# Half-tile sums, value tiles loaded once, and weight preparation moved: an attention, SiLU and squared-ReLU chain on one core

## The chip, the core and the metric

The kernel runs on one core of a Trainium2 chip. The metric is the device time of one execution in microseconds (us); lower is better. The core has a matrix engine (PE, TensorE), a vector engine (DVE), a scalar engine (ACT), GpSimd (POOL) and a sync engine (SP), which here issues nearly every transfer between HBM and the on-chip memory. Each engine works through its own instructions in the order in which they stand; an instruction that waits for another engine or for a transfer holds up everything behind it on its engine.

## The reference

```
def _attn_ref(q, k, v):                       # 4 batches, 8 heads, 576 positions, 64 wide
    ...
    mask = (rel >= 0) & (rel < window)        # window 128
    scores = np.where(mask, scores + bias[None], -1000000000.0)
    ...
    return np.matmul(attn, v)
def _moe_ref(x, w_in, w_out):                 # 2304 tokens, 512 -> 2048 -> 512
    h = x @ w_in
    g = h * (1.0 / (1.0 + np.exp(-h)))
    return g @ w_out
def _moe2_ref(x, w_in, w_out):                # the same sizes
    h = np.maximum(x @ w_in, 0.0)
    return h * h @ w_out
```

The output is the second layer applied to the first layer applied to the attention output, all in float32.

## The kernel before, in words

Every float32 operand of a large product is held as two parts, a high one (a rounded copy, written by ACT) and a low one (the difference, written by DVE or POOL), and a product is three matmuls: high by high, high by low, low by high. The 2304 tokens form four blocks of 512 (0 to 3) and one narrow block of 256 (4). The work has four phases; the code numbers its steps by n within each.

- **Phase one** (n from 0 to 71, `mm1`, L651 and L640) multiplies by the first layer's w_in. The attention of the later blocks is interleaved up to n = 55 (scores L303, transposes L387, values L433). Results pass `act1` on ACT and `act2` on DVE (L674) and are stored to HBM as `g0d`. Steps 64 to 71 work on the narrow block with two accumulators each, joined by ACT (L663) and DVE (L664).
- **Phase two** multiplies by the first layer's w_out. Blocks 0 and 1 do so directly (`mm2`, L815, n from 0 to 31): `load_g` fetches a piece of `g0d`, `split_g` makes its two parts (ACT L798, DVE L799), PE does twelve matmuls. Blocks 2 and 3 use seven products of sums instead of eight (`mm2_seven`, L746, pairs p from 16 to 31, two steps each); these need sums of w_out's quarters and of `g0d`. The narrow block follows directly (n from 64 to 71, L815 again).
- **Phases three and four** are the second layer in the same seven-product form (L875, then L970).

A weight tile `(layer, in or out, i)` is 1 MB. `prepare` takes one from HBM, repairs its words (`w_first` on DVE L482, `w_scale` on ACT L487, `w_join` on DVE L491), builds the quarter sums (`w_sums`, DVE L511 to L524) and stores the result back to HBM (`w_put`, L531, or `w_put_parts`, L555); a later phase gets it again (`w_get`, L538). For the first layer's w_out the parts are made at once (`w_hi`, and `w_lo` L502 on POOL) and stay on chip; its sums go to HBM in a whole 1 MB tile and come back in phase two, one tile at a time, into the single `raw` buffer, where `w_sums_hi` (ACT L588) and `w_sums_lo` (DVE L592) split them.

SP issues all transfers in the order of the code. A transfer also waits until the one eight places before it on the queue has landed, as the eight queue semaphores are used in turn.

Of the kernel before, what the change touches and what calls it, by code (L numbers as in the profile page):

```python
# [8 lines left out]
F32 = mybir.dt.float32  # L9
# [15 lines left out]
def kernel(  # L25
# [37 lines left out]
    wd0 = tc.dram_tile([P, NF // 2, 16 * P], F32, name="wd0")  # L63
# [41 lines left out]
    def attention(ap, ps, n0):  # L105
# [157 lines left out]
        def load_v(u):  # L263
            if double(u):
                return load_double_v(u)
            _, _, b, t0, n, m0, hp = units[u]
            t = ap.tile([P, 2, P], F32, tag="v", name="v", bufs=4)
            if m0 == n:
                nc.sync.dma_start(
                    out=t, in_=v[b, hp, t0 - m0:t0 + n, :].rearrange("(k p) d -> p k d", p=P)  # L270
                )
            else:
                if m0:
                    nc.sync.dma_start(out=t[:m0, 0], in_=v[b, hp, t0 - m0:t0, :])
                nc.sync.dma_start(out=t[:n, 1], in_=v[b, hp, t0:t0 + n, :])
            xv[u] = [t[:, 0], t[:, 1]]
# [222 lines left out]
    def w_lo(x, chunks=(0, 1)):  # L499
        w = w_t[x]  # L500
        for a in chunks:
# [7 lines left out]
    def w_sums(x):  # L509
# [9 lines left out]
        else:  # L519
# [4 lines left out]
            tt(low[:, 3], high[:, 0], low[:, 2], ALU.subtract)  # L524

# [205 lines left out]
    def mm2_seven(p, some_, pools):  # L731
# [4 lines left out]
            [ws_t[0, 1, i][:, y, 2 * P * j:2 * P * (j + 1)] for j in range(4)]  # L736
# [16 lines left out]
    def evacuate_second(b, step):  # L753

        acc = acc_t[0, b]
        c11, c12, u, c22 = e1
# [24 lines left out]
    def load_g(n):  # L781
        if n < NS:
            if "n" not in places:
                places["n"] = x_p.tile([P, 16 * P], F32, tag="xa", name="l")
            t = places["n" if n < 2 * FIRST else "l"][:, n % 4 * BLK:(n % 4 + 1) * BLK]
# [5 lines left out]
    def split_g(n):  # L791
        if n < NS:
            t, at_ = l_t.pop((0, n)), n % 3 * 2 * BLK
# [276 lines left out]
    def prepare(phase, x, place, n):  # L1070

        then(phase, n - 3, lambda: w_load(x, place(I32)))
        then(phase, n, w_first, x)
        then(phase, n, w_scale, x)
        then(phase, n + 1, w_join, x)
        then(phase, n + 2, w_sums, x)
# [6 lines left out]
        then(phase, n + 5, w_put_parts, x)  # L1083

# [12 lines left out]
    with tc.manual_schedule():  # L1097
# [5 lines left out]
        with tc.tile_pool(name="at", bufs=2) as ap, tc.tile_pool(  # L1103
# [511 lines left out]
```

## Time and profile before

| what | value |
| --- | --- |
| time, median of 3 runs | 883.37 us (881.88 to 885.65) |
| the profiled execution's own time | 881.42 us |
| its span, first to last instruction | 879.6 us |
| PE busy | 851.4 us (97%) |
| DVE busy, ACT busy, POOL busy | 619.4 us, 461.5 us, 135.9 us |
| mean granted PE clock, as a share of full speed | 0.992 |
| moved by DMA | 205.08 MB, 233 GB/s on average |

PE busy is the union of its matmuls; the ends of matmuls are modelled, so short waits between matmuls can hide in it. The granted clock is 1.00 (2.4 GHz) or 0.50 (1.2 GHz) at any moment; a window's figure is the mean.

### The profile page before, as it was taken

Reading aid. Unit: us, or ns where it says so; the run is one execution under the profiler, and the core shown is the slowest. Engines: PE = TensorE matmul, PEld = TensorE weight load, DVE = VectorE, ACT = ScalarE, POOL = GpSimd, SP = SyncE. Lnnn points to the kernel's source line nnn. Section 1 sums busy time; section 2 is a strip of 40 time slices with the busy share of each in tenths; the row PEclk is TensorE's granted clock in tenths of the full one; section 3 lists DMA queues with packets and bytes.
Section 4 is the critical chain, followed back from the end, with each engine's and each line's share of the span. In section 5 each row is a group of like instructions: output and inputs, shape, how many; then the busy total and the mean of one; then the engine's idle time right before and its main releaser. Section 6 shows DMA issues by size and latency. Waiting matters only on the chain.

```text
span 879.6 us, 17249 instructions
## 1 busy us (share of the span) xinstructions
PE 851.4 (97%) x6296; PEld 769.4 (87%) x6296; DVE 619.4 (70%) x1302; ACT 461.5 (52%) x925; POOL 135.9 (15%) x208
## 2 busy tenths in 40 slices
PE   8999999899999999998999799999999999999998
PEld 7678787687888887778999699999999999999998
DVE  6766686856765575667993356684957789998884
ACT  8788685657643553334332246665666543344331
POOL 6675432452631000000000000000000000000000
PEclk9999999999999999999999899999999999999999
DMA  9676799999967599993466826649477953444431
GB/s 276 205 228 206 222 326 312 311 363 324 341 233 251 178 345 415 400 348 123 142 224 232 287 72 206 226 168 321 165 250 271 313 192 127 151 140 144 132 109 48
DMA packets 126324, 205.08 MB, mean 233 GB/s; under 512 B 12704, under 2 KB 87712, under 8 KB 121632
## 3 DMA queue, kind: packets, MB, share of 16 engines
q1 hardware_dynamic: 125968, 203.86, 68.6%
q8 instruction: 49, 0.80, 0.4%
q14 instruction: 35, 0.29, 0.1%
q10 hardware_dynamic: 272, 0.13, 0.1%
HBM read 126.88 MB, written 77.07 MB: 232 GB/s over the span
## 4 chain that ended last, share of the span: by engine, by line
PE 78%; DMA 12%; DVE 5%; ACT 2%; issue 2%; SPq 1%; POOL 1%; DVEq 0%; ACTq 0%; POOLq 0%
PE acc L970 20%; PE h L651 18%; PE a L875 10%; PE acc L746 8%; DMA raw<-wd 5%; PE d L875 5%; PE acc L815 4%; PE b L875 3%; PE h L640 3%; PE o L433 2%; DMA spare<-in_w_dram 2%; PE s L303 1%; DMA l<-g0d 1%; PE so L303 1%; PE pp L387 1%
## 5 line engine op out<-in xcount | busy, mean ns | idle before, releaser
L651 PE MATMUL h<-x,w 128*128 128x512 f32 x768 | 184.8, 397 | 1.5 <-DVE t L674 1.5
L970 PE MATMUL acc<-w,g 128*128 128x256 f32 x1372 | 182.3, 283 | 1.0 <-DVE g L942 0.6
L970 PEld LDWEIGHTS acc<-w,g 128*128 128x128 f32 x1372 | 175.0, 192 | 1.6 <-DVE g L942 0.8
L651 PEld LDWEIGHTS h<-x,w 128*128 128x128 f32 x768 | 142.7, 189 | 35.9 <-DVE st L329 2.2
L815 PE MATMUL acc<-gx,w 128*128 128x512 f32 (+1 forms) x512 | 116.1, 387 | 8.8 <-DVE gx L799 7.2
L815 PEld LDWEIGHTS acc<-gx,w 128*128 128x128 f32 x512 | 93.6, 194 | 31.0 <-DVE gx L799 9.9
L935 ACT CAST g<-lay 128x1024 fp32r<-128x1024 f32 x36 | 37.9, 1052 | 96.0 <-issue 51.1
L875 PE MATMUL a<-x,w 128*128 128x384 f32 x432 | 80.9, 335 | 0.7 <-ACT t L1520 0.7
L356 POOL TENSOR_SCALAR z<-z,st 128x192 f32<-128x192 f32 (+1 forms) x104 | 65.3, 644 | 91.5 <-DVE st L350 47.3
L875 PEld LDWEIGHTS a<-x,w 128*128 128x128 f32 x432 | 75.3, 188 | 1.2 <-ACT t L1520 1.0
L674 DVE SCALAR_TENSOR_TENSOR t<-t,h 128x512 f32<-128x512 f32 x64 | 43.7, 683 | 27.3 <-ACT t L669 27.0
L669 ACT ACTIVATE t<-h 128x512 f32<-128x512 f32 x64 | 38.3, 598 | 37.6 <-PE h L651 35.8
L746 PE MATMUL acc<-x,w 128*128 128x256 f32 x392 | 56.1, 283 | 0.5 <-DVE lay L1024 0.5
L746 PEld LDWEIGHTS acc<-x,w 128*128 128x128 f32 x392 | 52.3, 192 | 0.8 <-DVE lay L1024 0.7
L339 ACT ACTIVATE z<-z,st 128x192 f32<-128x192 f32 (+1 forms) x104 | 45.5, 440 | 7.1 <-DVE st L329 7.0
L798 ACT CAST gx<-l 128x512 fp32r<-128x512 f32 x40 | 24.3, 623 | 42.6 <-DMA l<-g0d 29.7
L487 ACT ACTIVATE spare<-spare 128x1024 f32<-128x1024 f32 x25 | 29.2, 1166 | 26.6 <-DMA spare<-in_w_dram 26.6
L746 PE MATMUL acc<-g,w 128*128 128x256 f32 x140 | 40.4, 289 | 2.7 <-DVE g L724 2.7
L502 POOL TENSOR_TENSOR w<-spare,w 128x512 fp32r<-128x512 f32 x28 | 39.1, 1415 | 22.1 <-ACT w L497 22.0
L799 DVE TENSOR_TENSOR gx<-l,gx 128x512 fp32r<-128x512 f32 x40 | 27.4, 688 | 20.1 <-ACT gx L798 19.8
L970 PE MATMUL acc<-w,gx 128*128 128x256 f32 x140 | 39.6, 283 | 0.0
L942 DVE TENSOR_TENSOR g<-lay,g 128x1024 fp32r<-128x1024 f32 x26 | 31.9, 1225 | 9.2 <-ACT g L935 7.0
(195 smaller groups left out, 1469.0 us busy)
## 6 DMA issues: line engine op xcount, KB each, us to landing
g0d<-t SPq DMA_DIRECT2D x72, 256.0 KB, 5.9
lay<-g1d SPq DMA_DIRECT2D x72, 256.0 KB, 3.3
spare<-in_w_dram SPq DMA_DIRECT2D x34, 512.0 KB, 8.0
raw<-wd SPq DMA_DIRECT2D x15, 1024.0 KB, 7.0
wd<-spare SPq DMA_DIRECT2D x12, 1024.0 KB, 8.0
l<-g0d SPq DMA_DIRECT2D x40, 256.0 KB, 7.1
g1d<-t SPq DMA_DIRECT2D x50, 192.0 KB, 3.7
g1d<-lay SPq DMA_DIRECT2D x46, 192.0 KB, 3.8
```

The costliest lines, as they stand in the source:

```text
L339: nc.scalar.activation(z[r, j, k], z[r, j, k], AF.Exp, bias=least[r, j:j + 1], scale=-1.0, accum_out=total[r, j:j + 1],)
L356: nc.gpsimd.tensor_scalar(z[r, j, k], z[r, j, k], share[r, j:j + 1], 1.0, ALU.mult, ALU.mult)
L502: nc.gpsimd.tensor_tensor(w[:, 1, a], words(x)[1][:, a].bitcast(F32), w[:, 0, a].bitcast(F32), ALU.subtract)
L651: nc.tensor.matmul(h[:, j * w:(j + 1) * w], lhsT=wi[:, wh, c * P:(c + 1) * P], rhs=x[xh][:, c, :w], start=c == 0 and i == 0, stop=c == KC ...
L669: nc.scalar.activation(t_t[n], h_t[n], AF.Tanh, scale=0.5)
L674: nc.vector.scalar_tensor_tensor(t, t, 1.0, h, ALU.add, ALU.mult)
L746: nc.tensor.matmul(acc[name][:, m], lhsT=w[y][j][:, m * P:(m + 1) * P], rhs=g1[(p - FIRST) % 3][x][:, k], start=i == 0 and m == 0 and z == ...
L815: nc.tensor.matmul(to, lhsT=wo[:, a, c * P:(c + 1) * P], rhs=rhs, start=f == 0 and i == 0, stop=f == NF - 1 and i == len(both) - 1, skip_g ...
L875: nc.tensor.matmul(acc[to], lhsT=w[wh][:, c * P:(c + 1) * P], rhs=o[:, xh, c], start=r in (0, 1, 3) and c == 0 and k == 0, stop=c == 1 and ...
L935: nc.scalar.copy(g[0][:, :, :4], l_t[1, d])
L942: tt(g[1][:, :, :4], a, g[0][:, :, :4].bitcast(F32), ALU.subtract)
L970: nc.tensor.matmul(acc[to][:, half], lhsT=g[x], rhs=w[y], start=i == 0 and half == 0 and j == 0, stop=i == NI - 1 and j == 2, skip_group_c ...
```

## The change

- The sums of the first layer's w_out are written as a half tile over the upper half of the raw tile, in another order, and kept as 512 KB. Phase two gets them two at a time, side by side in one `raw` buffer (`get_sums` at n = 3, 9, 15 and 21, used at 7 and 8, 13 and 14, 18 and 19, 25 and 26). `w_lo` of these tiles becomes one DVE instruction in place of two on POOL.
- Value tiles of the attention are loaded one 128 by 128 block at a time and a block is used by both units that need it. A unit issues one transfer as before, of 64 KB in place of 128 KB for 36 units.
- Five weight tiles are prepared near the end of phase one: (0,1,7) as before, and (1,0,4) to (1,0,7), of which two were prepared in mid phase one and two in phase two. They lie in `raw` and in the buffers `lay` and `gx`, whose pools now open at n = 55 in place of after phase one.
- Loads of weight tiles are asked four or five steps ahead of use in place of three. `load_l`, the sums and parts for the seven products, `load_g` of the narrow block, `split_g` of it and `load_x2` stand earlier in the code; slots of buffers are renumbered to allow it. In phase three the preparation of (1,1,5), (1,1,6) and (1,1,7) moves by 6, 7 and 1 steps.

The core of the diff (block indentation that only moved is left out):

```
-    wd0 = tc.dram_tile([P, NF // 2, 16 * P], F32, name="wd0")
+    wd0 = tc.dram_tile([P, NF // 2, 8 * P], F32, name="wd0")
...
+            for t in (t0 - m0, t0):
+                if (b, hp, t) not in c:
+                    c[b, hp, t] = ap.tile([P, P], F32, tag="v", name="v", bufs=8)
+                    nc.sync.dma_start(out=c[b, hp, t], in_=v[b, hp, t:t + P, :])
+            xv[u] = [c[b, hp, t] for t in (t0 - m0, t0)]
...
     def w_lo(x, chunks=(0, 1)):
         w = w_t[x]
+        if x[1]:
+            nc.vector.tensor_tensor(
+                w[:, 1], words(x)[1].bitcast(F32), w[:, 0].bitcast(F32), ALU.subtract
+            )
+            return
...
+            s = sums_of(x)
+            tt(s[:, 0], high[:, 3], high[:, 2], ALU.subtract)
+            tt(s[:, 1], high[:, 3], high[:, 1], ALU.subtract)
+            tt(s[:, 2], high[:, 1], s[:, 0], ALU.subtract)
+            tt(s[:, 3], high[:, 0], s[:, 2], ALU.subtract)
...
+    def get_sums(x, at):
+        sums_t[x] = at.bitcast(F32)
+        nc.sync.dma_start(out=sums_t[x], in_=kept(x))
...
-            for x, n, raw in (
-                ((1, 0, 0), 16, spare), ((1, 0, 1), 19, spare), ((1, 0, 4), 21, own),
-                ((1, 0, 2), 23, spare), ((1, 0, 3), 27, spare), ((1, 0, 5), 30, own),
-                ((0, 1, 0), 32, spare), ((0, 1, 1), 35, spare), ((0, 1, 2), 38, own),
-                ((0, 1, 3), 42, spare), ((0, 1, 4), 45, spare), ((0, 1, 5), 49, spare),
-                ((0, 1, 6), 53, spare), ((0, 1, 7), 59, own),
-            ):
+        for x, *when in (
+            ((1, 0, 0), 12), ((1, 0, 1), 15, 20), ((1, 0, 2), 18, 23), ((1, 0, 3), 22, 27),
+            ((0, 1, 0), 26, 31), ((0, 1, 1), 30, 35), ((0, 1, 2), 34, 38), ((0, 1, 3), 38, 42),
+            ((0, 1, 4), 41, 45), ((0, 1, 5), 45, 49), ((0, 1, 6), 49, 53),
+        ):
+            prepare(x, spare, 1, *when)
+        for x, place, *when in (
+            ((0, 1, 7), own, 56, 59), ((1, 0, 4), in_l, 56, 61), ((1, 0, 5), in_gx, 57, 63),
+            ((1, 0, 6), own, 65, 69), ((1, 0, 7), in_l, 67, 71),
+        ):
+            prepare(x, place, 1, *when)
...
-            for x, n in (
-                ((1, 1, 4), 1), ((1, 0, 6), 5), ((1, 0, 7), 8), ((1, 1, 0), 11), ((1, 1, 1), 15),
-                ((1, 1, 2), 18), ((1, 1, 3), 22),
-            ):
+        for x, *when in (
+            ((1, 1, 4), -2, 2), ((1, 1, 0), 3), ((1, 1, 1), 7), ((1, 1, 2), 11), ((1, 1, 3), 15),
+        ):
+            prepare(x, spare, 2, *when)
...
-            for i, n in enumerate((3, 7, 10, 14, 17, 21, 25, 29)):
+        for i, n, n1 in (
+            (0, 3, 7), (1, 3, 8), (2, 9, 13), (3, 9, 14), (4, 15, 18), (5, 15, 19), (6, 21, 25),
+            (7, 21, 26),
+        ):
...
-                if n == 2 * FIRST - 8:
+            if n == 2 * FIRST - 11:
                     for p in range(3):
                         load_l(FIRST + p)
...
-                if 2 * WIDE - 5 <= 2 * p:
-                    load_g(2 * p + 4)
-                    load_g(2 * p + 5)
-                if p == WIDE - 1:
+            if p in (WIDE - 5, WIDE - 3):
+                load_g(p + WIDE + 5)
+                load_g(p + WIDE + 6)
+            if p == WIDE - 2:
                     split_g(2 * WIDE)
...
-                split_g(n + 1)
+            split_g(n + 2)
```

The new `prepare(x, place, phase, first, n)` loads at step `first`, then runs `w_first` and `w_scale` at n, `w_join` at n + 1, `w_sums` at n + 2 and `w_put` at n + 3; n is `first + 4` where it is not given.

What moves, in the order of the program's own instructions, at three places.

**The vector engine where phase one ends and phase two begins.** Before, from `act2` of step 70 on (`t<-t,lay` is `act2`, `lay<-h,lay` the join of step 71, `gx<-l,gx` a `split_g`, `spare<-spare` the first step on weight tile (1,1,4)):

```order
L674 SCALAR_TENSOR_TENSOR t<-t,lay 128x512
L664 TENSOR_TENSOR lay<-h,lay 128x256 x2
L799 TENSOR_TENSOR gx<-l,gx 128x512
L674 SCALAR_TENSOR_TENSOR t<-t,lay 128x512
L799 TENSOR_TENSOR gx<-l,gx 128x512 x2
L482 TENSOR_SCALAR spare<-spare 128x1024
L799 TENSOR_TENSOR gx<-l,gx 128x512
```

With the change, from the join of step 70 on (L678 is the join, L688 `act2`, L813 `split_g`; `raw<-raw` works on tile (1,0,6), `lay<-lay` on tile (1,0,7)):

```order
L678 TENSOR_TENSOR lay<-h,lay 128x256 x2
L486 SCALAR_TENSOR_TENSOR raw<-raw 128x1024
L813 TENSOR_TENSOR gx<-l,gx 128x512
L688 SCALAR_TENSOR_TENSOR t<-t,lay 128x512
L678 TENSOR_TENSOR lay<-h,lay 128x256 x2
L515 TENSOR_TENSOR raw<-raw 128x256
L516 TENSOR_TENSOR raw<-raw 128x256
L517 TENSOR_TENSOR raw<-raw 128x256
L518 TENSOR_TENSOR raw<-raw 128x256
L477 TENSOR_SCALAR lay<-lay 128x1024
L813 TENSOR_TENSOR gx<-l,gx 128x512
```

And right behind these:

```order
L688 SCALAR_TENSOR_TENSOR t<-t,lay 128x512
L486 SCALAR_TENSOR_TENSOR lay<-lay 128x1024
L515 TENSOR_TENSOR lay<-lay 128x256
L516 TENSOR_TENSOR lay<-lay 128x256
L517 TENSOR_TENSOR lay<-lay 128x256
L518 TENSOR_TENSOR lay<-lay 128x256
L813 TENSOR_TENSOR gx<-l,gx 128x512 x3
L477 TENSOR_SCALAR spare<-spare 128x1024
```

Before, the second `split_g` stands directly behind the join of step 71 and two more right behind `act2`. Now the four sums of (1,0,6) and the first step on (1,0,7) stand ahead of the second `split_g`, and the join and the four sums of (1,0,7) ahead of the third.

**The sync engine at the same seam.** Before, from step 71 of phase one on (`g0d<-t` are stores of phase one, `l<-g0d` loads for `split_g`, `raw<-wd_74` a whole tile of sums, `spare<-in_w_dram` a weight tile):

```order
L679 DMA g0d<-t 128x2x256
L786 DMA l<-g0d 128x512
L679 DMA g0d<-t 128x2x256 x2
L786 DMA l<-g0d 128x512 x2
L538 DMA raw<-wd_74 128x2048
L786 DMA l<-g0d 128x512 x2
L474 DMA spare<-in_w_dram 128x1024 x2
L786 DMA l<-g0d 128x512 x2
L538 DMA raw<-wd_74 128x2048
```

With the change (`wd<-raw` and `wd<-lay` put the tiles (1,0,6) and (1,0,7)):

```order
L693 DMA g0d<-t 128x2x256
L800 DMA l<-g0d 128x512
L693 DMA g0d<-t 128x2x256
L543 DMA wd<-raw 128x2048
L693 DMA g0d<-t 128x2x256
L543 DMA wd<-lay 128x2048
L800 DMA l<-g0d 128x512 x5
L469 DMA spare<-in_w_dram 128x1024 x2
L598 DMA raw<-wd_74 128x1024 x2
L800 DMA l<-g0d 128x512 x4
```

Two puts of 1 MB that wait for DVE's sums now stand ahead of the loads `l<-g0d` for steps 4 to 7, and two half tiles of sums are loaded behind step 8's load.

**The sync engine where the seven products end and the narrow block begins.** Before (`l<-g0d` of 128x2x256 are the narrow loads, `w<-hd` parts of w_in for phase three, `lay<-x2d` operands for phase three, `x2d<-lay` results of the last pair):

```order
L786 DMA l<-g0d 128x2x256 x2
L834 DMA lay<-x2d 128x2x384 x2
L1031 DMA x2d<-lay 128x2x256
L786 DMA l<-g0d 128x2x256 x2
L580 DMA w<-hd 128x1024
L580 DMA w<-hd 128x768
L580 DMA w<-hd 128x1024
L580 DMA w<-hd 128x768
L834 DMA lay<-x2d 128x2x384
L786 DMA l<-g0d 128x2x256
L1031 DMA x2d<-lay 128x2x256 x3
L786 DMA l<-g0d 128x2x256
```

With the change:

```order
L800 DMA l<-g0d 128x2x256 x2
L589 DMA w<-hd 128x1024
L589 DMA w<-hd 128x768
L589 DMA w<-hd 128x1024
L589 DMA w<-hd 128x768
L800 DMA l<-g0d 128x2x256 x2
L589 DMA w<-hd 128x1024
L589 DMA w<-hd 128x768
L589 DMA w<-hd 128x1024
L589 DMA w<-hd 128x768
L848 DMA lay<-x2d 128x2x384 x3
L1045 DMA x2d<-lay 128x2x256
```

Before, the third and fourth narrow loads stand behind the first store of the last pair's results, which waits for DVE; now four narrow loads stand ahead of that store, with parts of w_in between and behind them.

## Rows read from the trace of the kernel before

**Rows 1.** Busy time by engine in stretches of the span (windows).

```profile
core 0: us, PE busy (x) PEld busy (x) DVE busy (x) ACT busy (x) POOL busy (x), PEclk, DMA share, GB/s
...
139.00:202.00 63.00, 57.89 (x516) 45.17 (x515) 42.25 (x133) 38.83 (x99) 23.84 (x34) 0.97 0.98 339
...
305.40:398.40 93.00, 89.85 (x386) 71.51 (x385) 60.70 (x91) 39.97 (x55) 0.00 (x0) 1.00 0.96 366
...
398.40:416.00 17.60, 14.42 (x105) 13.97 (x105) 12.67 (x21) 7.84 (x10) 0.00 (x0) 0.90 0.44 149
...
484.00:508.00 24.00, 18.30 (x86) 15.43 (x86) 10.83 (x16) 5.67 (x9) 0.00 (x0) 0.86 0.80 263
...
508.00:691.00 183.00, 181.70 (x1046) 179.94 (x1045) 122.64 (x194) 110.07 (x208) 0.00 (x0) 1.00 0.64 219
```

**Rows 2.** Timeline, attention stretch: start, length, engine, line, [idle before, releaser].

```profile
151.09 0.70 DVE L482 TENSOR_SCALAR spare<-spare 128x1024 int32<-128x1024 uint32 x1 [6.07 <-DMA spare<-in_w_dram]
...
154.72 3.04 PE L651 MATMUL h<-x,w 128*128 128x512 f32 x12 [1.48 <-DVE t L674]
...
200.05 0.88 PE L303 MATMUL so<-k,q 64*64 64x192 f32 x16 [1.37 <-ACT pt L400]
```

**Rows 3.** Line 474, the weight loads: who waited for them (us, times).

```profile
  DVE spare L482: 20.3, 9
```

**Rows 4.** Line 538, the loads of kept tiles: who waited, and landing times.

```profile
  ACT w L588: 16.4, 7
...
DMA to landing us min/median/max: 4.6/6.8/10.1
```

**Rows 5.** Timeline of PE in the second product, wide part.

```profile
375.98 3.31 PE L815 MATMUL acc<-gx,w 128*128 128x512 f32 x12 [0.84 <-DVE gx L799]
...
412.37 0.58 PE L746 MATMUL acc<-g,w 128*128 128x256 f32 x1 [2.70 <-DVE g L724]
```

**Rows 6.** Timeline at the seam of the first and second product.

```profile
303.18 0.42 DVE L664 TENSOR_TENSOR lay<-h,lay 128x256 f32<-128x256 f32 x1 [0.67 <-ACT lay L663]
...
305.41 16.96 PE L815 MATMUL acc<-gx,w 128*128 128x512 f32 x74
...
306.54 0.69 DVE L799 TENSOR_TENSOR gx<-l,gx 128x512 fp32r<-128x512 f32 x1
...
307.14 0.69 DVE L674 SCALAR_TENSOR_TENSOR t<-t,lay 128x512 f32<-128x512 f32 x1
```

**Rows 7.** DVE steps of one weight tile: ns min/median/max, first and last start.

```profile
L482 DVE TENSOR_SCALAR spare<-spare x25: 665/698/1497, 16.9 to 377.1; 128x1024 int32<-128x1024 uint32 x25
...
L491 DVE SCALAR_TENSOR_TENSOR spare<-spare x25: 1195/1221/1739, 21.1 to 379.4; 128x1024 int32<-128x1024 int32 x25
...
L515 DVE TENSOR_TENSOR spare<-spare x6: 396/420/489, 108.3 to 336.4; 128x256 f32<-128x256 f32 x6
...
L518 DVE TENSOR_TENSOR spare<-spare x6: 420/535/584, 109.6 to 337.5; 128x256 f32<-128x256 f32 x6
...
L592 DVE TENSOR_TENSOR w<-raw,w x8: 1220/1225/1226, 317.1 to 397.7; 128x1024 fp32r<-128x1024 f32 x8
```

**Rows 8.** The narrow part: PE's timeline, and one piece of the chain.

```profile
486.48 13.09 PE L815 MATMUL acc<-gx,w 128*128 128x512 f32 x64 [2.14 <-DVE gx L799]
...
503.13 7.05 PE L815 MATMUL acc<-gx,w 128*128 128x512 f32 x30 [3.56 <-DVE gx L799]
...
484.27 3.20 DMA l<-g0d
```

**Rows 9.** DMA: two windows, the page's rate by slice, one issue.

```profile
140.00:250.00 110.00, 104.89 (x953) 83.56 (x952) 73.20 (x222) 70.19 (x180) 47.41 (x67) 0.98 0.99 337
...
264.00:305.40 41.40, 41.40 (x212) 35.18 (x211) 21.88 (x36) 17.11 (x33) 2.84 (x2) 1.00 0.62 207
...
GB/s 276 205 228 206 222 326 312 311 363 324 341 233 251 178 345 415 400 348 123 142 224 232 287 72 206 226 168 321 165 250 271 313 192 127 151 140 144 132 109 48
...
l<-g0d SPq DMA_DIRECT2D x40, 256.0 KB, 7.1
```

More of the change, by code (lines that the diff above doesn't have):

```diff
@@ L1068, in own, with prepare @@
         return raw_p.tile([P, 16 * P], dtype, tag="raw", name="raw")
-    def prepare(phase, x, place, n):
-        then(phase, n - 3, lambda: w_load(x, place(I32)))
+    def prepare(x, place, phase, first, n=None):
+        n = first + 4 if n is None else n
+        then(phase, first, lambda: w_load(x, place(I32)))
         then(phase, n, w_first, x)
@@ L1075, in prepare @@
         then(phase, n + 1, w_join, x)
+        if x[0] == 0:
+            then(phase, n + 1, w_hi, x)
+            then(phase, n + 2, w_lo, x)
         then(phase, n + 2, w_sums, x)
@@ new lines @@
+        load_k_strip(0, slice(0, 1))
+        load_q_apart(0)
+        wake()
+        load_k_strip(0, slice(1, NHP))
+        constants()
+        biases(0)
+        load_q_apart(1)
+        load_k_strip(1)
+        load_v_strip(0)
+        zs = []
+        for _ in range(3):
+            z = spare(F32)[:, :3 * 2 * 5 * 64].rearrange("p (i a c) -> p i a c", i=3, a=2)
+            zeros(z)
+            zs += [z[:, i] for i in range(3)]
+        load_q_apart(2)
+        load_k_strip(2)
+        load_v_strip(1)
@@ new lines, in steps, with some @@
+        def steps(n, some_=(1, 2, 3, 4, 0)):
+            for k in some_:
+                for x in at(n, k):
+                    (w_first, w_scale, w_join, w_hi, w_lo)[k](x)
+        def some(*us):
+            return [u for u in us if u < NU]
+        for n in range(-3, 0):
+            w_loads(n)
+        visits = {n: [(), (), ()] for n in range((NB - 1) * NF)}
+        for n in range(4, (NB - 1) * NF, 4):
+            u = n0 + n
+            visits[n][2] = some(*range(u, u + 4))
+            visits[n + 3][0] = some(*range(u - 4, u))
+            visits[n + 3][1] = some(*range(u, u + 4))
@@ new lines @@
+        for d in range(7, NS // 2):
+            then(4, 2 * d - 4, sums_a, d)
+            then(4, 2 * d - 4, hi_a, d)
+            then(4, 2 * d - 3, lo_a, d)
+            then(4, 2 * d - 3, load_a, d + 3)
+        for n in range((NB - 1) * NF, NS + 3):
+            if n < NS:
+                mm1(n)
+            if 0 < n <= NS:
+                act1(n - 1)
+                act2(n - 1)
+            join(n, lay[:, 28 * P:])
+            store_t(n - 2)
+            do(1, n)
+            if NS - 4 <= n < NS:
+                load_g(n - (NS - 4))
+            if n == NS - 2:
+                gx = x3["gx"] = gp_.tile([P, 24 * P], F32R, tag="gx", name="gx", bufs=1)
+            if NS - 2 <= n < NS:
+                split_g(n - (NS - 2))
+            if n == NS - 2:
+                do(2, -2)
@@ L1569 @@
+        squares()
+        store_halves(first + waiting)
+        do(4, -1)
+        for n in range(NS):
+            if n < NS - 2:
+                seven(accs, n)
+            elif n == NS - 2:
+                seven(accs, n, n + 1)
+            do(4, n)
+            if seq[n][1] == NI - 1:
+                evacuate_seven(seq[n][0])
+            elif n > 1 and seq[n - 2][1] == NI - 1:
+                store_all()
+        store_all()
 _OUTS = [((2304, 512), 'float32')]
```

815 lines of the change are left out of this document (373 added, 442 removed).

## Prediction

> **What bounds the kernel now.** I read the page first: PE is busy nearly all the time, so what a change can win is what PE loses. The losses were then found with windows cut where the phases change [rows 1]; in each, the window's length less PE's busy time is open idle time, and one less the granted clock, times the length, is what half speed took.
>
> - 139 to 202 us, attention inside phase one: 63.0 - 57.9 = 5.1 idle, and 0.03 x 63 = 1.9 at half speed.
> - 305.4 to 398.4, the direct products of phase two: 386 matmuls, each 16.96 / 74 = 0.229 us in an undisturbed run [rows 6], need 88.4 of 93.0, so 4.6 is lost. Only 3.15 shows as idle; the rest hides in modelled ends.
> - 398.4 to 416, the start of the seven products: 3.2 idle, and 0.10 x 17.6 = 1.8 at half speed.
> - 484 to 508, the narrow block: 5.7 idle, and 0.14 x 24 = 3.4 at half speed.
> - 508 to 691, phase three: 1.3 idle.
>
> Together 27.0 us. Then I asked the timeline what ended each wait. In the attention stretch DVE stood 6.07 us before the first step on a weight tile, whose transfer was late; PE's wait of 1.48 for DVE and its wait of 1.37 for ACT follow from such stops [rows 2]. Over the kernel DVE waited nine times, 20.3 us, for weight tiles loaded into spare buffers [rows 3]. In phase two ACT waited seven times, 16.4 us, for tiles of sums [rows 4]: there is one buffer, so a tile can be asked for only when the one before is split. PE's waits of 0.84 and 2.70 are for DVE work that queued behind this [rows 5]. In the narrow block PE waited 2.14 and 3.56 us for `split_g`, and the chain names the load before it, which left only at 484.27, when the seven products were already over [rows 8].
>
> **The change part by part.** *Attention.* The prepared tiles (1,0,4) and (1,0,5) leave this stretch: a load and a put of 1 MiB each, 4 MiB. Five puts of sums halve, 2.5 MiB. Of 36 halved value loads some 20 fall here, 1.25 MiB. The stretch moved 337 GB/s over 110 us [rows 9], 37.1 MB; 7.75 MiB or 8.1 MB fewer leave 29.0, that is 264 GB/s. The loads that remain are asked one or two steps earlier. The waits of rows 2 are waits for late loads, so I take back nearly all of the 7.0. `w_lo` moves from POOL to DVE: 1.22 us as the like operation of L592 [rows 7], eight times, seven of them while attention runs. DVE is busy 42.25 of 63 us there [rows 1], so most is covered; without that cover all eight are 9.8. I charge 0.8; bounds 0 and 9.8.
>
> *The seam.* Here the moved work lies badly. The order shows what DVE runs between the joins and the splits. In the trace the last join of step 70 ends at 303.18 + 0.42 = 303.60 [rows 6]. From there DVE now has, without a gap: `w_join` 1.22, `split_g` 0.69, `act2` 0.69, two joins 0.84, four sums of 0.42 to 0.53, say 1.9, `w_first` 0.70, `split_g` 0.69 [rows 6, 7], 6.7 in all: the second split ends at 310.3. PE's first direct step, from 305.41, takes 12 x 0.229 = 2.75 and ends at 308.2, so PE waits 2.2. Then `act2`, `w_join`, the sums of (1,0,7) and a split are 4.5 more: 314.8, against PE's next end at 313.1, another 1.7. That is 3.9. A wait of 2.14 was followed by half speed in the narrow block [rows 1, 8]. If it comes after the first wait it is hidden in the second; if later it costs the 1.8 of the stretch at 412. I add half, 0.9, so 4.8; bounds 0 (joins and steps run ahead) and 3.9 + 3.4. The loads for steps 4 to 7 now stand behind the put that waits for DVE until about 314.2; with a landing of 4.6, the quickest of rows 4, they arrive at 319, and after ACT's and DVE's parts step 4 can start at about 320.4, just when PE comes there (314.9 + 2 x 2.75). Late next is thus this load, if it lands later.
>
> *Direct products.* Two tiles (load and put, 4 MiB) and half of eight loads of sums (4 MiB) leave a stretch that ran at 366 GB/s [rows 1]; two puts come in. 93 us of that are 34.0 MB; 6 MiB or 6.3 MB less leave about 27.7. The sums are asked three to five steps ahead, and two at once, so the chain of one buffer is cut. I keep 0.8 of the 4.6; bounds 0 and 4.6. At the start of the seven products the last sums are split at step 26, where before step 29 was named and the tile came late, and the operands are made two steps earlier: I keep 0.3 of 5.0 (bounds 0 and 5.0).
>
> *Narrow block.* Four loads now stand ahead of the store that held them, and two splits are done before PE comes. The fifth load waits behind a store and 1.75 MiB of parts. By the 366 GB/s of rows 1 these take 5 us, with the store's wait of some 3 the load lands about 8 us into the block, and its matmuls start after four steps of over 2.7 us, at 11. I keep 1.0 of 9.1; bounds 0 and 9.1.
>
> *Phase three.* Tile preparation moves off the steps in which operands are made: I keep 0.4 of 1.3 (bounds 0 and 1.3). Nothing else in phases three and four changes place.
>
> The sum: 27.0 less 0.8 + 4.8 + 0.8 + 0.3 + 1.0 + 0.4 = 8.1 is a gain of 18.9. The profiled execution took 881.4, so its like takes 862.5. The median shown is 1.95 above the profiled one; I carry half of that and forecast **863.5**.
>
> **A rule weighed.** The page's slices ran up to 415 and 400 GB/s [rows 9], both inside the direct products. The end of phase one, 264 to 305.4, ran at 207 GB/s, 8.6 MB [rows 9]; four loads and two puts more, and two halved puts, add 5 MiB, which makes 13.8 MB or 334 GB/s. By the peak there is room of a fifth. The Trainium skill (DMA: Bandwidth & Descriptors, Specifications) puts the HBM limit of one core at about 358 GB/s; by that rule the end of phase one and the seam would have hardly any room, and the time would be the first rival's 873.5. The trace disagrees with it as a limit for one slice.
>
> **The rivals.**
>
> - *Piled-up transfers.* If the end of phase one runs near what the queue gives, the two puts at the seam (2.1 MB, 6 us at 350 GB/s) delay steps 4 to 7 in full, and the direct products keep 4.0 more of their loss: 863.5 + 6 + 4 = 873.5. For it: landings of up to 10.1 us [rows 4]. Against it: 0.62 of DMA share there before, and the peak.
> - *DVE in phase one.* If each `w_lo` delays the release of an accumulator by its length, 9.0 more: 872.5. For it: PE does wait for `act2` [rows 2]. Against it: there the cause was a late transfer, and three accumulators give two steps of slack.
> - *A quiet seam.* DVE catches up, no wait: 863.5 - 4.8 = 858.7. Against it stands the order of the instructions.
> - *Nothing leaves sooner.* SP still reaches each load when the work ahead of it is done, so the attention keeps its 7.0 and the direct products their 4.6, on top of the seam and the 6 us pile-up: 863.5 + 6.2 + 3.8 + 6 = 879.5.
> - *Slower.* Place: `load_g` in the direct products. Step n + 5's load leaves when step n's slot is free and must land within three steps, 8.25 us; before, the issue took 7.1 at the median [rows 9]. If the late start at the seam is never made up because the median landing rises, each of 32 steps waits for the excess. From 9.0 us on, 0.75 a step, this costs 24 and decides: 887.5.
>
> **How the numbers follow.** Chances: the forecast 0.60 (its own range 858 to 869), piled-up transfers 0.15, DVE in phase one 0.09, quiet seam 0.08, nothing leaves sooner 0.05, slower 0.03. From 855, below the quiet seam by its unknown rest, to 875, beyond the first two rivals, the range leaves out the last two cases and the tails of the others, under 2 in 10. A change of less than 0.5%, 4.4 us, can hardly be told from none. Faster by more: 0.60 + 0.15 + 0.09 + 0.08 = 0.92; within: the fifth case, 0.05; slower 0.03.
>
> **What would show it.** Right: DVE's waits at weight loads in mid phase one gone and PE's idle time there under 1 us; a PE wait of about 2 and one of under 2 us within 10 us of the first direct matmul, both for `split_g` on DVE; no ACT wait for sums over 3 us; no PE wait and full clock at the narrow block. Wrong: PE waits at the seam for a transfer and not for DVE; new waits for `act2` between steps 31 and 62 of phase one; a median landing of `load_g` above 9 us.

## The result and the profile after

| what | before | after |
| --- | --- | --- |
| time, median | 883.75 us (881.88 to 885.65, 4 runs) | 856.65 us (854.4 to 859.1, 4 runs) |
| ratio, 95% interval | | 0.9694 (0.9659 to 0.9729) |
| the profiled execution's own time, its span | 881.42 us, 879.6 us | 857.31 us, 855.5 us |
| PE busy in the span | 851.4 us | 840.9 us |
| moved by DMA | 205.08 MB | 194.34 MB |

The change made the kernel 27.1 us faster; 863.5 was forecast, with a range of 855 to 875. Windows of the changed kernel, cut at the first matmul of each part (phase one, direct products, seven products, narrow block, phase three, phase four):

```profile
core 0: us, PE busy (x) PEld busy (x) DVE busy (x) ACT busy (x) POOL busy (x), PEclk, DMA share, GB/s
0.00:298.47 298.47, 291.72 (x2592) 235.36 (x2593) 210.14 (x652) 204.72 (x531) 114.45 (x192) 1.00 0.80 260
298.47:389.01 90.54, 88.37 (x386) 71.77 (x385) 63.91 (x98) 39.77 (x56) 0.00 (x0) 1.00 0.86 315
389.01:469.65 80.64, 80.64 (x674) 80.63 (x673) 61.56 (x96) 29.68 (x35) 0.00 (x0) 1.00 0.61 200
469.65:493.52 23.87, 22.77 (x131) 19.49 (x129) 14.20 (x20) 7.89 (x14) 0.00 (x0) 1.00 0.65 226
493.52:668.35 174.83, 174.83 (x1008) 174.83 (x1009) 119.57 (x191) 108.51 (x204) 0.00 (x0) 1.00 0.66 231
668.35:855.50 187.15, 182.58 (x1513) 181.60 (x1512) 154.62 (x265) 69.79 (x88) 0.00 (x0) 1.00 0.44 141
```

From 389 to 668 us PE waits only once, for 1.10 us, and no part of phases two and three runs at half speed; before, the start of the seven products ran at 0.90 and the narrow block at 0.86 [rows 1]. The same cuts in all profiled executions, before and after and the kernels of the next section (us; each column is the time from the first matmul of one part to that of the next):

| kernel | phase one | direct | seven | narrow | phase three | phase four to end | median us |
| --- | --- | --- | --- | --- | --- | --- | --- |
| before | 305.41 | 93.05 | 88.02 | 29.50 | 176.75 | 186.83 | 883.75 |
| after | 298.47 | 90.54 | 80.64 | 23.87 | 174.83 | 187.19 | 856.65 |
| late asking (e1) | 300.38 | 90.49 | 80.63 | 23.88 | 174.84 | 189.02 | 860.04 |
| two tiles back (e2) | 303.46 | 90.48 | 80.63 | 24.19 | 174.85 | 187.28 | 863.99 |
| old value loads (e3) | 297.07 | 90.75 | 80.63 | 25.40 | 174.83 | 186.76 | 856.64 |
| one half tile at a time (e4) | 297.95 | 90.64 | 80.63 | 24.73 | 174.86 | 186.43 | 856.50 |
| narrow loads as before (e5) | 298.17 | 91.56 | 82.93 | 23.46 | 174.85 | 188.64 | 857.94 |
| whole tiles of sums (e6) | 299.10 | 103.45 | 80.63 | 23.98 | 174.86 | 186.16 | 867.58 |
| before, asked sooner (e7) | 303.26 | 97.58 | 87.77 | 30.37 | 176.73 | 186.16 | 881.05 |
| mended (e8) | 299.16 | 90.35 | 80.63 | 23.92 | 174.83 | 186.51 | 855.10 |
| mended, put sooner (e9) | 298.02 | 87.10 | 80.63 | 24.19 | 174.83 | 186.44 | 852.37 |
| late asking and tiles back (e10) | 306.25 | 90.48 | 80.64 | 24.42 | 174.85 | 186.23 | 865.00 |
| before, half tiles of sums (e11) | 303.34 | 87.77 | 84.46 | 29.30 | 176.70 | 188.39 | 871.74 |

So the 24.0 us between the two spans came from phase one (6.9), the direct products (2.5), the seven products (7.4), the narrow block (5.6) and phase three (1.9); phase four gave back 0.4. In the changed kernel, e4, e5, e8 and e9, whose edits leave nearly all of phase one alone, it ends between 297.95 and 299.16: so much is chance. The direct products of the old kernel vary more: 93.05 in its own profile and 97.58 in e7, whose edit leaves their steps alone.

Who waited for the weight loads (line 469 now) in the changed kernel (us, times), to be set against 20.3 us in nine waits [rows 3]:

```profile
  DVE raw L477: 2.7, 1
```

And for the sums (line 598), against 16.4 us in seven [rows 4]:

```profile
  ACT w L602: 1.4, 1
```

DVE's nine waits for weight tiles in spare buffers are gone, and in the attention stretch PE stands still nowhere. The window from 140 to 250 us, in which PE was busy for 104.89 us at 337 GB/s before [rows 9]:

```profile
140.00:250.00 110.00, 110.00 (x1027) 88.94 (x1027) 80.89 (x234) 74.86 (x185) 34.10 (x57) 1.00 0.86 281
```

The forecast was 264 GB/s; PE does 1027 matmuls in this window where it did 953, so the transfers of more steps fall into it. PE's timeline at the seam, and at the narrow block:

```profile
298.47 3.17 PE L829 MATMUL acc<-gx,w 128*128 128x512 f32 x13
302.41 3.01 PE L829 MATMUL acc<-gx,w 128*128 128x512 f32 x12 [0.77 <-DVE gx L813]
306.34 5.53 PE L829 MATMUL acc<-gx,w 128*128 128x512 f32 x23 [0.92 <-DVE gx L813]
312.13 0.51 PE L829 MATMUL acc<-gx,w 128*128 128x512 f32 x1 [0.26 <-ACT gx L812]
312.86 1.43 PE L829 MATMUL acc<-gx,w 128*128 128x512 f32 x5 [0.22 <-DVE gx L813]
...
469.65 22.77 PE L829 MATMUL acc<-gx,w 128*128 128x512 f32 x128
493.52 0.80 PE L889 MATMUL a<-x,w 128*128 128x384 f32 x3 [1.10 <-DVE lay L1036]
```

The two waits for `split_g` came where they were forecast, but shorter; then come two short ones, for the two parts of one split whose load left late. The narrow block's 128 matmuls run without a wait (2.14 and 3.56 before [rows 8]); behind it phase three waits 1.10 for the evacuation of an accumulator.

### The profile page after: what moved, and what is told of

The parts are those of the page before. It is cut to its first block, busy times and chain, and to the rows that moved or that the text cites. A ratio compares the mean times of both kernels' runs of the same rounds, so it can differ in the third digit from the quotient of the medians.

```text
span 855.5 us, 17230 instructions
## 1 busy us (share of the span) xinstructions
PE 840.9 (98%) x6296; PEld 763.7 (89%) x6296; DVE 624.0 (73%) x1318; ACT 460.4 (54%) x925; POOL 114.4 (13%) x192
## 2 busy tenths in 40 slices
DMA packets 121717, 194.34 MB, mean 227 GB/s; under 512 B 12704, under 2 KB 83104, under 8 KB 119072
## 4 chain that ended last, share of the span: by engine, by line
PE 83%; DMA 6%; DVE 5%; issue 2%; SPq 2%; ACT 2%; POOL 0%; DVEq 0%; ACTq 0%; POOLq 0%
PE h L665 18%; PE acc L984 17%; PE a L889 11%; PE acc L760 9%; PE acc L829 9%; PE d L889 5%; PE o L428 3%; PE b L889 3%; PE h L654 2%; DMA l<-g0d 1%; PE so L298 1%; DMA k<-in_k_dram 1%; DMA g0d<-t 1%; PE pp L382 1%; PE pp L298 1%
## 5 line engine op out<-in xcount | busy, mean ns | idle before, releaser
L829 PE MATMUL acc<-gx,w 128*128 128x512 f32 (+1 forms) x512 | 111.3, 378 | 2.2 <-DVE gx L813 1.9
L829 PEld LDWEIGHTS acc<-gx,w 128*128 128x128 f32 x512 | 91.3, 188 | 21.7 <-DVE gx L813 3.3
L688 DVE SCALAR_TENSOR_TENSOR t<-t,h 128x512 f32<-128x512 f32 x64 | 43.6, 683 | 29.8 <-ACT t L683 27.8
L813 DVE TENSOR_TENSOR gx<-l,gx 128x512 fp32r<-128x512 f32 x40 | 27.5, 688 | 35.9 <-ACT gx L812 35.7
L486 DVE SCALAR_TENSOR_TENSOR spare<-spare 128x1024 int32<-128x1024 int32 x24 | 29.8, 1243 | 7.5 <-ACT spare L482 7.5
L324 DVE CUSTOM_DVE_ANT_0 z<-so,bias 128x192 f32<-128x192 f32 (+2 forms) x60 | 17.1, 326 | 17.2 <-PE so L298 15.2
```

The costliest lines, as they stand in the source:

```text
L486: nc.vector.scalar_tensor_tensor(high, high, 3, low, ALU.logical_shift_left, ALU.bitwise_or)
L688: nc.vector.scalar_tensor_tensor(t, t, 1.0, h, ALU.add, ALU.mult)
L829: nc.tensor.matmul(to, lhsT=wo[:, a, c * P:(c + 1) * P], rhs=rhs, start=f == 0 and i == 0, stop=f == NF - 1 and i == len(both) - 1, skip_g ...
```

## Experiments

Ratios are to the kernel before on the same chip, with 95% intervals; the changed kernel stands at 0.9694.

**Attention: asked sooner, or fewer bytes?** First the asking alone is undone (e1):

```
-            prepare(x, spare, 1, *when)
+            n = when[1] if len(when) > 1 else when[0] + 4
+            prepare(x, spare, 1, n - 3, n)
```

> The changed kernel, with one thing undone: the eleven weight tiles of mid phase one are asked three steps ahead of use again, in place of four or five. Bytes and order of all else stay. Theory A, asking: the waits of the attention stretch (7.0 us before) went because the loads leave sooner. Then about 6 of the 7 us come back: first direct matmul near 304.5 us of the span in place of 298.5, time about 863 against 856.7. Theory B, bytes: they went because 4 MiB and more left the stretch, so that a load lands in time even when asked late. Then less than 1 us comes back: 856 to 858, and PE's idle time from 27 to 278 us stays under 1 us (none in the changed kernel).

Measured: 860.04, ratio 0.9731 (0.9706 to 0.9756). Phase one took 1.9 us more; another 1.8 lies in phase four, which the edit does not touch. Who waited for the weight loads (us, times):

```profile
  ACT spare L482: 8.1, 2
  DVE spare L477: 6.7, 2
```

Some waits are back, but PE feels only part of them: neither theory's number. The ratio's interval overlaps that of the changed kernel, so the time alone does not show the loss. Then the two tiles go back into mid phase one (e2):

```
-            ((0, 1, 7), own, 56, 59), ((1, 0, 4), in_l, 56, 61), ((1, 0, 5), in_gx, 57, 63),
+            ((1, 0, 4), own, 17, 21), ((1, 0, 5), own, 26, 30), ((0, 1, 7), own, 56, 59),
```

> The changed kernel, with the tiles (1,0,4) and (1,0,5) prepared in mid phase one again (asked at steps 17 and 26, used from 21 and 30, in the raw buffer) and no longer in late phase one; 4 MiB of loads and puts go back into the attention stretch, the other loads keep their sooner asking. Theory B, bytes: most of the 7.0 us comes back, some 4 to 6, so 861 to 863, DVE waits of over 2 us for weight loads there, and over 330 GB/s in that stretch against 307 in the changed kernel. Theory A, asking: less than 1 us, 856 to 858. If both are needed, this run and the one with late asking each give back 1 to 4 us.

Measured: 863.99, ratio 0.9779 (0.9753 to 0.9805), phase one 5.0 longer. PE's timeline shows where:

```profile
187.61 0.44 PE L428 MATMUL o<-pt,v 128*64 128x128 f32 x4
191.08 1.24 PE L428 MATMUL o<-pt,v 128*64 128x128 f32 x14 [3.02 <-DMA v<-in_v_dram]
```

Not a weight tile but a small value load is late, which left behind a put of each of two tiles and a load of 1 MB, and the next 4 us run at a clock of 0.58. The size was that of the theory of bytes, the place was not: DVE's waits for weight loads did not return, and the stretch moved 313 GB/s. The edit also brings the tiles' work on ACT and DVE back, so it does not show the bytes alone. Both undone together, with the same two edits and the two tiles, too, asked three steps ahead (e10):

> The changed kernel, with both parts of the attention undone: tiles (1,0,4) and (1,0,5) back in mid phase one, and all the loads there asked three steps ahead. Each alone gave back some: late asking about 2 us of phase one, the two tiles about 5. If both causes add: phase one ends at about 305.5, where it ended before, and the time is 863.5 to 866. If one lateness covers the other: phase one ends at 303 to 304, 862 to 864.

Measured: 865.00, ratio 0.9792 (0.9754 to 0.9829), phase one ends at 306.25 us, the whole former loss and a little more. Its timeline, a row of DVE and one of PE:

```profile
169.93 0.70 DVE L477 TENSOR_SCALAR spare<-spare 128x1024 int32<-128x1024 uint32 x1 [7.66 <-DMA spare<-in_w_dram]
...
173.52 2.02 PE L665 MATMUL h<-x,w 128*128 128x512 f32 x5 [3.89 <-DVE t L688]
```

That is the chain of [rows 2] again: a late weight tile stops DVE, and PE waits for `act2` behind it. 1.9 and 5.0 are 6.9 together, 7.8 was measured: in phase one of these profiles the two causes add. The medians show it less well: 3.4 and 7.3 us longer alone, 8.4 together.

In the kernel before, 2.1 us of PE's waits in this stretch ended on POOL, and the change takes `w_lo` off POOL. That is not what helped: e11 (below), with `w_lo` on DVE, has the same waits as before. The longest of them, before and in e11:

```profile
163.23 0.37 PE L387 MATMUL pp<-ident,z 64*128 64x64 f32 x2 [1.36 <-POOL z L356]
...
160.87 0.27 PE L387 MATMUL pp<-ident,z 64*128 64x64 f32 x2 [1.37 <-POOL z L356]
```

The reverse test gives the asking alone to the kernel before (e7):

```
-                prepare(1, x, raw, n)
+                prepare(1, x, raw, n, 3 if raw is own else 4 if x[2] == 0 else 5)
```

(the new last argument is the number of steps ahead)

> The kernel before, with one thing of the change: the weight tiles of mid phase one that lie in spare buffers are asked four or five steps ahead of use in place of three. Bytes stay. Theory A, asking: the attention stretch gains 2 to 6 us, 878 to 882. Theory B, bytes: with 337 GB/s moved there already, a load asked sooner waits among the same transfers, under 1.5 us is gained, 882.5 to 885. If it is both together, neither alone gives what the sum gives.

Measured: 881.05, ratio 1.0012 (0.9981 to 1.0042). Its profile has phase one 2.2 us shorter and the direct products 4.5 longer, though the edit leaves their steps alone; in the time, asking alone gained nothing that can be measured. Last, the value loads as before (e3: the old `load_v` with its tile of 128 by 256 in place of the shared blocks):

> The changed kernel, with value tiles loaded as before, 128 KB a unit in place of 64 (some 1.25 MiB more in the attention stretch, 2.25 MiB in all). Theory B, bytes, in proportion: 1.25 of the 7.75 MiB that left the stretch, so about 1.1 of the 7.0 us comes back, 857.8. Theory A, asking, or slack in the stretch: nothing, 856 to 857.5, no PE wait from 27 to 278 us.

Measured: 856.64, ratio 0.9696 (0.9673 to 0.9720): nothing. PE has no wait from 27 to 276 us. What a part of the bytes is worth is not in proportion: 1.25 MiB more in this stretch changed nothing that can be seen.

**Direct products: the chain of one buffer, or the bytes?** One half tile at a time, three steps from asking to use (e4):

```
-            (0, 3, 7), (1, 3, 8), (2, 9, 13), (3, 9, 14), (4, 15, 18), (5, 15, 19), (6, 21, 25),
-            (7, 21, 26),
+            (0, 3, 7), (1, 7, 10), (2, 10, 13), (3, 13, 16), (4, 16, 19), (5, 19, 22), (6, 22, 25),
+            (7, 25, 28),
...
-                get_sums(x, places["s"][:, x[2] % 2 * 8 * P:][:, :8 * P])
+                get_sums(x, own()[:, :8 * P])
```

> The changed kernel, with the half tiles of sums got one at a time into the single buffer, each asked when the one before has been split and used three steps later (7, 10, 13, ... 28), as before; the bytes stay halved. Theory C, the chain of one buffer: the direct products and the start of the seven products lose again, ACT waits for sums over 8 us in all, 3 to 6 us come back, 860 to 863. Theory B, bytes: a half tile lands within its three steps (8.3 us) nearly always, ACT waits under 3 us in all for sums, and under 1 us comes back, 856 to 858.

Measured: 856.50, ratio 0.9701 (0.9675 to 0.9726). The chain is back, and ACT waits; PE loses nothing by it. Waits for line 598 (us, times), and the window of the direct products:

```profile
  ACT w L602: 10.7, 5
```

```profile
297.95:388.59 90.64, 88.35 (x387) 71.81 (x385) 63.87 (x98) 39.56 (x56) 0.00 (x0) 1.00 0.86 315
```

The same, with whole tiles of 1 MB kept and fetched (e6: `wd0` of 16 * P, `kept(x)` put and fetched whole, the sums read from its upper half):

> The changed kernel, with the sums of w_out kept as whole tiles of 1 MB again (8 puts in phase one and 8 loads in phase two of 1 MB in place of 512 KB), got one at a time with three steps between, as in the kernel before. The run with half tiles got one at a time showed that the chain of one buffer alone costs nothing. Theory B, bytes: the direct products and the start of the seven products lose part of their former 9.6 us again, and phase one a little: 3 to 7 us, 860 to 864, ACT waits over 12 us for sums. Theory E, neither the chain nor the bytes of the sums held the direct products: under 1 us, 856 to 858; then what was late there was the preparation of two more tiles in phase two, or the order of steps around the start of the seven products.

Measured: 867.58, ratio 0.9859 (0.9823 to 0.9895). The same two views:

```profile
  ACT w L602: 25.3, 7
```

```profile
299.10:402.55 103.45, 93.41 (x387) 73.33 (x385) 63.79 (x98) 39.78 (x56) 0.00 (x0) 0.97 0.86 314
```

The direct products take 12.9 us longer than in the changed kernel, of which half speed took 0.03 x 103 = 3; phase one changes little, the seven products not at all. That is more than was expected, and more than the kernel before lost. The bytes and the chain cost together what the chain alone does not: a tile of 1 MB with three steps of time (8.2 us) landed 4.9 to 9.9 us after its issue. A likely reason why e6 loses more than the kernel before, read from the trace and not tested: it asks for a tile in the same step in which the one before is split, and SP stood 17.6 us before these loads until a tile had landed (2.9 in the kernel before), with the loads for `split_g` behind it. And the reverse: the kernel before, with half tiles alone (e11: `sums_of`, the half put, `get_sums` one at a time at the old steps, `w_lo` on DVE):

> The kernel before with one part of the change: sums of w_out kept and fetched as half tiles (with their low parts made by DVE), still one at a time at the old steps. 2.5 MiB leave the attention stretch and 4 MiB the direct products. Theory B, bytes in time (a tile must land within its three steps): the direct products, which lost 6.0 us against a pitch of 2.72 us a step, lose under 2; ACT waits for sums fall from 16.4 to under 8 us; phase one gains 1 to 3; in all 5 to 8 us, 876 to 879 where the kernel before has 883.7. Rival, two tiles prepared in phase two: they hold the direct products, which still lose 4 or more, and 2 us or less are gained in all, 882 to 884.

Measured: 871.74, ratio 0.9853 (0.9817 to 0.9888), more than the theory said. The same two views (the sums' load is line 604 here):

```profile
  ACT w L608: 9.9, 5
```

```profile
303.34:391.11 87.77, 87.55 (x386) 72.00 (x385) 62.60 (x94) 41.10 (x57) 0.00 (x0) 1.00 0.91 339
```

Against the profile of before, phase one is 2.1 shorter, the direct products 5.3, the seven products 3.6, though two weight tiles are still prepared in phase two: the rival falls. Halving the sums is the largest single part of the gain that an experiment shows: 10.8 us against the kernel before on the same chip, the move of `w_lo` included.

**The narrow block.** Loads and splits at their old places (e5):

```
-            if p == WIDE - 1:
-                split_g(2 * WIDE + 1)
...
-            if p in (WIDE - 5, WIDE - 3):
-                load_g(p + WIDE + 5)
-                load_g(p + WIDE + 6)
-            if p == WIDE - 2:
+            if 2 * WIDE - 5 <= 2 * p:
+                load_g(2 * p + 4)
+                load_g(2 * p + 5)
+            if p == WIDE - 1:
                 split_g(2 * WIDE)
...
-            split_g(n + 2)
+            split_g(n + 1)
```

> The changed kernel, with the loads and splits of the narrow block where they stood before (two loads behind each of the last pairs, the first split after the last pair, the others one step ahead). Theory D, place in the queues: the waits of 2.14 and 3.56 us and some 3.4 us of half speed come back, 6 to 9 us, 863 to 866, with PE waits for the split at the narrow block. Theory B, bytes: those loads came late because the stretch was crowded; with fewer bytes elsewhere they land in time, under 2 us comes back, 856 to 858.5.

Measured: 857.94, ratio 0.9748 (0.9712 to 0.9784).

```profile
472.66 11.56 PE L829 MATMUL acc<-gx,w 128*128 128x512 f32 x64 [2.14 <-DVE gx L813]
484.86 1.31 PE L829 MATMUL acc<-gx,w 128*128 128x512 f32 x6 [0.64 <-DVE gx L813]
```

The first wait comes back to the hundredth of a microsecond. It was the order on DVE: the two loads had landed by 469.54, and the splits stood behind the evacuation of the seven products. Of the second, 3.56 before, 0.64 is left, and half speed does not follow. In the table, seven products and narrow block together are 1.9 us longer, where the change had won 13.0 in them.

Why the second wait did not come back is read from DVE's timeline, before and in e5. The first row of each is a sum of phase three's operands, the second the split that PE waits for:

```profile
501.52 0.96 DVE L842 TENSOR_TENSOR lay<-lay 128x768 f32<-128x768 f32 x1 [9.04 <-DMA lay<-x2d]
502.40 0.68 DVE L799 TENSOR_TENSOR gx<-l,gx 128x512 fp32r<-128x512 f32 x1
...
482.77 0.96 DVE L856 TENSOR_TENSOR lay<-lay 128x768 f32<-128x768 f32 x1 [5.64 <-DMA lay<-x2d]
484.11 0.69 DVE L813 TENSOR_TENSOR gx<-l,gx 128x512 fp32r<-128x512 f32 x1 [0.38 <-ACT gx L812]
```

Before, DVE stood 9.04 us for the last `lay<-x2d` load, issued at 497.86, with a split behind it whose own load had landed at 496.43. The sum starts 15.0 us behind the block's first matmul before, and 10.1 in e5: the change asks for this load (`load_x2`) two steps sooner, and e5 leaves that alone. The halved sums are not it, since e11, which asks at the old step, has 3.25 us there. No run tried `load_x2` by itself. The 0.64 left in e5 is the wait for the block's fifth load, and it is no mark of the old places: e3, e4, e8, e9 and e10, which load the block as the changed kernel does, have 0.18 to 1.13 us there. The ratio says 0.5% and the medians 0.15%, on different chips.

**The seam, mended.** The preparation steps go behind the splits and the loads, (1,0,6) a step sooner, (1,0,7)'s DVE steps into phase two, and the narrow block is evacuated ahead of the last operand conversion (e8):

```
-            ((1, 0, 6), own, 65, 69), ((1, 0, 7), in_l, 67, 71),
+            ((1, 0, 6), own, 64, 68),
...
+        then(1, 67, lambda: w_load((1, 0, 7), in_l(I32)))
+        for n, what in ((0, w_first), (0, w_scale), (1, w_join), (2, w_sums), (3, w_put)):
+            then(2, n, what, x)
...
             store_t(n - 2)
-            do(1, n)
             if NS - 4 <= n < NS:
                 load_g(n - (NS - 4))
...
                 split_g(n - (NS - 2))
+            do(1, n)
...
             store_all()
+            if n == NS - 1:
+                evacuate(lay[:, 28 * P:], NB - 1)
             do(2, n)
-        evacuate(lay[:, 28 * P:], NB - 1)
```

> The changed kernel, mended in two places: at the seam of phases one and two the preparation steps stand behind the splits and loads, tile (1,0,6) one step sooner and (1,0,7)'s DVE steps in the first steps of phase two; and the narrow block's sums are evacuated ahead of the last operand conversion. Theory S, queue order on DVE: the seam's waits of 0.77, 0.92, 0.26 and 0.22 us and the 1.10 us at the start of phase three go, no new wait comes: 853 to 854. Rival, transfers: PE waits at the seam for a load instead, over 1 us, or the puts that now come later delay loads of steps 4 to 8: 856 to 859.

Measured: 855.10, ratio 0.9711 (0.9675 to 0.9747), no difference that can be told. The seam's waits are gone, and the 1.10 us at the start of phase three is down to 0.53. The direct products take 90.4 us as before the mending, since new waits came:

```profile
299.16 24.67 PE L829 MATMUL acc<-gx,w 128*128 128x512 f32 x108
324.05 0.50 PE L829 MATMUL acc<-gx,w 128*128 128x512 f32 x1 [0.22 <-ACT gx L812]
324.77 6.48 PE L829 MATMUL acc<-gx,w 128*128 128x512 f32 x25 [0.23 <-DVE gx L813]
...
377.99 3.04 PE L829 MATMUL acc<-gx,w 128*128 128x512 f32 x12 [0.34 <-DVE gx L813]
381.44 8.23 PE L829 MATMUL acc<-gx,w 128*128 128x512 f32 x35 [0.41 <-DVE gx L813]
```

The loads behind the first of them were issued from 314.25 on, after the put of (1,0,7), a weight tile and two half tiles, all between 310.7 and 313.6, and landed up to 9.6 us later. So the put was moved out of this burst, and the tile's DVE steps with it (e9):

```
-        for n, what in ((0, w_first), (0, w_scale), (1, w_join), (2, w_sums), (3, w_put)):
+        then(1, 71, w_first, x)
+        then(1, 71, w_scale, x)
+        for n, what in ((0, w_join), (1, w_sums), (1, w_put)):
             then(2, n, what, x)
```

> The mended kernel with one more edit: tile (1,0,7)'s DVE steps start at the last step of phase one and its put leaves at step 1 of phase two, where it left at step 3 among a burst of loads. In the mended kernel the seam's waits were gone, but steps 8 to 11 of the direct products lost 1.6 us to loads that landed 8 to 9.6 us after their issue. Theory F, the burst: with the put out of it these land within their three steps, steps 8 to 11 go at 2.72 us each, and the direct products take 88 to 89 us against 90.4 there and 90.5 in the changed kernel. Theory B, bytes: the direct products move the same bytes at a full queue, and the loss turns up elsewhere in them: 90 to 90.6 again. In time 853 to 855 by the first, 855 to 857 by the second.

Measured: 852.37 (851.31 to 853.00, 6 runs), ratio 0.9641 (0.9610 to 0.9673), faster than the kernel before and than e8, whose interval on the same chip lies above. All its times lie below all of the changed kernel's, but the two intervals overlap by a little. The window of its direct products:

```profile
298.02:385.12 87.10, 87.10 (x386) 72.07 (x385) 63.09 (x96) 39.96 (x56) 0.00 (x0) 1.00 0.89 336
```

No wait is left in them, with the same bytes as in e8. So the sum of the bytes did not hold them. How much was the burst is shown only in part: of the 3.25 us that e8 lost, some 1.4 lie in steps 8 to 11 behind the burst; the rest lies in steps 22, 28 and 29, 60 us and more into the part. Waits at step 28 or 29 stand in e5 and e6, too, and not in e4 and the changed kernel, and no experiment names their cause. 87.10 is thus what 384 matmuls need.

## Why the prediction was right, point by point

- **Attention, 6.2 forecast, 6.9 measured.** Late loads were the cause (e2, e10). Of the means named, the two tiles count most, 5.0 us of phase one (e2); sooner asking is worth some 2 in single profiles (e1, e7), which the times do not show. The value loads gave nothing (e3), and whole sums cost phase one of the changed kernel 0.6 (e6), which is within chance. The charge of 0.8 for `w_lo` on DVE was not needed: no PE wait from 27 to 278 us, and 0.34 for `act2` right behind. That also settles the rival of DVE in phase one.
- **Seam, 4.8 forecast, 3.4 measured** (90.54 - 87.10). The mechanism was right, the sizes were not. DVE's chain from the join of step 70 to the second split took 302.36 - 296.69 = 5.7 us and not 6.7: the four sums took 1.7 and not 1.9, and the rest is that DVE's instructions overlap (last section). PE also had one matmul of the next step to do before it stood. So the two waits show as 0.77 and 0.92 idle, and with 0.2268 us for each matmul between the starts they cost 1.0 and 1.2, not 2.2 and 1.7. The 0.9 for half speed did not come. The load behind the put, named as next late, was the third wait: issued at 306.12, it landed 5.24 us later, and cost 1.1 us that the sum had at nothing.
- **Direct products, 3.8 forecast, 5.9 measured** (93.05 - 87.10, without the seam). Two steps failed. The loss of before was taken as 4.6 from a mean of 0.229 us a matmul in a row of 74, in which modelled ends are counted; 87.10 / 384 is 0.2268. And 0.8 was kept on the argument that the chain of one buffer is cut: the chain costs nothing when the tiles are halved (e4), and the halves alone win all but 0.7 (e11).
- **Start of the seven products and narrow block, 12.8 forecast, 13.0 measured.** That these agree is luck in part. The prediction put the block's two waits down to a load that left at 484.27. The first was for splits queued behind the evacuation on DVE, the second for a sum that waited for `lay<-x2d` (e5's section), which the change cured by `load_x2`, a move that the prediction does not name. The 1.0 kept for a late fifth load did not come in the profile of the changed kernel, though five others have 0.18 to 1.13 of it; in its place stands a wait of 1.10 for the evacuation behind the block.
- **Phase three, 0.9 forecast, 1.9 measured**; phase four, which was left out, lost 0.4.
- **From span to median.** The sum was 18.9 against 24.0 in the spans. 1.0 was carried for the median above the profiled execution; after, the median lies 0.7 below its own. 5.1 + 1.0 + 0.7 are the 6.8 us between 863.5 and 856.65.
- **Rivals.** The quiet seam's 858.7 is nearest to the time, but the seam was not quiet; the other terms were too small. Piled-up transfers did not come in the changed kernel, beyond that third wait at the seam; e8 shows that a put at another step moves such waits, and does not remove them. The rates by slice on the changed kernel's page, to be set against the last row of [rows 9]:

```profile
GB/s 264 198 224 205 230 274 287 283 312 284 303 137 282 359 307 385 384 234 151 99 253 263 248 169 273 201 189 251 213 228 284 315 149 145 134 146 127 148 103 47
```

The end of phase one, where the moved tiles are loaded, runs at 282 and 359 GB/s (slices 13 and 14) without a wait of PE for a transfer; the direct products still reach 385 and 384. The Trainium skill (DMA: Bandwidth & Descriptors, Specifications) gives about 358 GB/s as one core's HBM limit; the direct products of both kernels ran above it for slices of 21 to 22 us, so the trace disagrees with it here.

## What to carry to other kernels

Count a transfer's time against the steps between its issue and its use, in the stretch where it runs: a wait of ACT for 10.7 us cost nothing as long as it stayed inside that slack, and 25.3 us of the same wait cost 12.9. When waits vanish at one place, look where the burst went: the mended seam gained only after one put of 1 MB had been moved out of a group of loads, though that put does not explain all of the gain. Follow a wait back through the order of its engine: the second wait at the narrow block was not for its own load, but for another one's, ahead of it on DVE. Fewer bytes gained at three places at once here; asking sooner alone gained nothing in the time that can be measured.

## What the runs showed of the hardware

DVE's instructions overlap, by the times of the profile. Its timeline in the changed kernel, start and duration:

```profile
296.60 1.22 DVE L486 SCALAR_TENSOR_TENSOR raw<-raw 128x1024 int32<-128x1024 int32 x1
297.73 0.69 DVE L813 TENSOR_TENSOR gx<-l,gx 128x512 fp32r<-128x512 f32 x1
298.33 0.69 DVE L688 SCALAR_TENSOR_TENSOR t<-t,lay 128x512 f32<-128x512 f32 x1
298.94 0.75 DVE L678 TENSOR_TENSOR lay<-h,lay 128x256 f32<-128x256 f32 x2
299.60 0.42 DVE L515 TENSOR_TENSOR raw<-raw 128x256 f32<-128x256 f32 x1
300.05 0.43 DVE L516 TENSOR_TENSOR raw<-raw 128x256 f32<-128x256 f32 x1
300.40 0.42 DVE L517 TENSOR_TENSOR raw<-raw 128x256 f32<-128x256 f32 x1
300.73 0.42 DVE L518 TENSOR_TENSOR raw<-raw 128x256 f32<-128x256 f32 x1
301.07 0.69 DVE L477 TENSOR_SCALAR lay<-lay 128x1024 int32<-128x1024 uint32 x1
301.67 0.69 DVE L813 TENSOR_TENSOR gx<-l,gx 128x512 fp32r<-128x512 f32 x1
```

Each next one starts some 0.09 us before the one ahead has ended (1.22 long, 1.13 to the next start; 0.69 and 0.60), so a chain is shorter than the sum of its durations; between the first two sums alone the step was 0.45.

Half speed did not follow every wait: after 2.14 us at the narrow block the granted clock fell in the kernel before (0.61 from 486.48 to 490.00) and stayed at 1.00 in e5; after 3.02 us in e2 it fell to 0.58 for 4 us.
